# A state-space layer beside a dense Mish layer: the second block's first projection takes eight more tiles as seven products, its stages take turns, and its skip product goes to GpSimd

## The chip, the cores and the metric

The kernel runs on one core of a Trainium2 chip. The core has five engines that take their instructions in order, each from its own queue: TensorE (PE in the profile, with its weight loads as PEld), VectorE (DVE), ScalarE (ACT), GpSimd (POOL) and SyncE (SP), which only issues transfers (DMAs). They wait for each other through semaphores. The metric is the device time of one execution in microseconds (us). Before the change it is 592.89 us, the median of three runs (592.56 to 593.47).

## What is computed

The input x has 2048 rows of 1024 numbers (bf16). Each row is normalised to xn. Two layers are applied to xn and added to x:

```python
x = A_x
xn = _layernorm(x)
# A: a diagonal complex recurrence over the 2048 rows
Lam_bar = exp(exp(log_dt) * Lam)
Bu = xn @ B_bar.T                      # complex, 1024 states
h[t] = Lam_bar * h[t-1] + Bu[t]
A = 2 * real(h @ Cmat.T) + xn * Dskip  # xn * Dskip is the "skip product"
# B: a dense layer, 1024 -> 3584 -> 1024
g = xn @ w1 + b1
B = (g * tanh(softplus(g))) @ w2       # the activation is Mish
out = x + A + B
```

## The kernel before

The 2048 rows are taken in four blocks of 512, `blk` 0 to 3; the change is about `blk` 1, the second, which the code calls `FAST`. A block has these stages on TensorE: the *first projection* xn @ w1 (28 tiles of 128 columns, f = 0 to 27), the *input projection* xn @ B (eight groups j of 128 states, real and imaginary part), and the *second projection*, act @ w2, with the output product h @ C behind it in the same PSUM banks.

A plain tile of the first projection (`first_tile`, matmuls at L839) is eight matmuls of 128x512; ScalarE takes it out of PSUM with Mish (L847). A tile can also be taken as part of *seven products*: four tiles (a *quad*) by 1024 input rows by 512 block rows are cut in halves each way, and seven products of halves replace eight. Each of the seven, a *unit*, is eight matmuls of 128x256 (`w_product`, L984). Four of the seven need sums of weight quarters (`w_sums`, VectorE, L1134) and sums of xnT quarters (`sums_x`, VectorE, L1645, kept in `TT`). The scaled weights and the sums are written to DRAM (`wsd`) by DMAs from GpSimd's queue (`w_store`, L1113) and come back through the ring. After a unit its bank is copied or joined (`w_evacuate`: ScalarE L1004, VectorE L1007 and the joins L1021), and Mish follows later over four tiles at a time (`mish`, L862). The input projection is done the same way in pairs of groups, a, b, c and d, with the sums of B made on VectorE (`sums_B`, L1639, after `scale_B`, L1626) and held in SBUF; its products are at L914, its copies at L929, L931, L956 and L958, its joins at L939.

In `blk` 1 before: `TILES` are 20 plain tiles, and `OPEN` takes quads p and q (8 tiles, 14 units). `WHOLE` then does the input projection. These orders are written out by hand as strings, which `project_fast` reads one word at a time: a letter and a number.

- `a2`, `b1`, `c5`: product 2, 1, 5 of the input projection for pair a, b, c. Product 1 opens bank X, 2 opens Y and 5 opens Z; 6, 7 and 4 add to X, 3 adds to Z, and each of these must wait until what the bank held is copied or joined.
- `p1`, `q5`, `s2`, `w4`: the same for a quad of the first projection. `W_BANKS` names the three banks.
- `r0` to `r7`: `rotate_in(j)` on VectorE, three instructions (L877, L883, L885): a turn of 1.22 us and two of 0.42, each with two SBUF tensors.
- `k0`: one of the weight sums that are waiting in `steps`, with its store. `v5`: scale group 5's weights (ScalarE, L1119) and queue its sums. `n0`: load group 0's raw weights (GpSimd's queue, L1058). `P0`: one part of `sums_B(3)`. `g4`: one Mish pass. `l`: loads the next block's x (L390).
- `u4` to `u7`: the first rows of the second projection for one output bank (six matmuls, L1391).

The recurrence is done by `recur` on VectorE (two scans L1353 and a rotation per group). The skip product of `blk` 1 is `ln_skip` (VectorE, L590 and L592, eight instructions), called between the plain tiles by `side(f)`. The next block's row statistics are made by ScalarE (`next_stats`, L568 to L572), which writes into xn.

The *ring* has seven slots of 512 KB. Its loads are issued by SP in the fixed order of `items` (L440 for w1, w2 and C, L437 for pairs of units from `wsd`); each waits for its slot and, for units, for the stores of what it reads. `item_done` emits the next load each time an item is used up. All queues are emitted in the order in which the program calls the helpers, so what stands earlier in a queue holds up what stands behind it.

Of the kernel before, what the change touches and what calls it, by code (L numbers as in the profile page):

```python
# [5 lines left out]
ALU = mybir.AluOpType  # L6
# [3 lines left out]
P = 128  # L10
# [153 lines left out]
def build_kernel(nc, A_x, A_Lambda_re, A_Lambda_im, A_B_re, A_B_im, A_C_re, A_C_im,  # L164
# [18 lines left out]
    SPLIT = range(2, NB)  # L183
    GROUPS = ((0, 7), (7, NPL), (NPL, NPL + 8), (NPL + 8, NF), (12, 16), (16, 20))
# [17 lines left out]
    OPENS = [(REAL[QUADS.index(o[0])], int(o[1])) for o in OPEN.split() if o[0] in QUADS]  # L202
    O_ITEMS = [("w1", f // 2) for f in TILES[::2]] + [("ws", tuple(OPENS[i:i + 2])) for i in range(0, len(OPENS), 2)]

# [90 lines left out]
    srow = act[:, 24:26, :].rearrange("p f t -> p (f t)")  # L295
    srow0 = act[:, 26:28, :].rearrange("p f t -> p (f t)")
    base_st = nc.lookup_mloc(st).addr
# [288 lines left out]
    def ln_skip(blk, q):  # L586
# [241 lines left out]
    def item_done():  # L828
        n_item[0] += 1
        ring_load()  # L830

# [57 lines left out]

    def product(pr, n):  # L890

        X, Y, Z = (4 * ((pr + 1) % 2) + i for i in range(3))
        js = (2 * pr, 2 * pr + 1)
        lo, hi = slice(0, TH), slice(TH, TB)
        raw = {1: (0, 0, lo), 2: (0, NH, lo), 4: (1, NH, None), 3: (None, NH, hi)}
        bank = {1: X, 6: X, 7: X, 4: X, 2: Y, 5: Z, 3: Z}[n]
        opens = n in (1, 2, 5)
        for j in js:
            for k in range(NH):
                if n in (1, 2, 4):  # L900
                    w = BT[:, raw[n][0], j, raw[n][1] + k, :]
                    b_w = b_BT[j]
                elif n == 7:
                    w, b_w = BT16[:, 1, j, k, :], b_BT[j]
                else:
                    w, b_w = SS[:, j, {5: 0, 6: 1, 3: 2}[n], k, :], b_CT[j]
                if n in (1, 2, 3):
                    x, b_x = xnT[:, raw[n][1] + k, raw[n][2]], b_xnT
                else:
                    t = {5: 0, 6: 1, 7: 2, 4: 3}[n]  # L910
                    x, b_x = TT[:, t, k, :], [b_xn[t]]
# [52 lines left out]
    def w_product(blk, i, n):  # L964
        X, Y, Z = W_BANKS[i]
# [3 lines left out]
        s, half = n_item[0] % NRING, units.index((REAL[i], n))  # L969
        unit = ring[:, s, half * 1024:(half + 1) * 1024]  # L970
        if n not in (1, 2, 4):
            unit = unit.bitcast(f16)
        for j in range(2):
            for k in range(NH):
                if n in (1, 2, 3):
                    t0 = TH if n == 3 else 0
                    x, b_x = xnT[:, (0 if n == 1 else NH) + k, t0:t0 + TH], b_xnT
                else:
                    t = {5: 0, 6: 1, 7: 2, 4: 3}[n]
                    x, b_x = TT[:, t, k, :], [b_xn[t]]  # L980
                w = unit[:, k * 2 * P + j * P:k * 2 * P + (j + 1) * P]
# [8 lines left out]
    def w_evacuate(blk, i, n, keep):  # L990
        X, Y, Z = W_BANKS[i]
        at = REAL[i]
# [43 lines left out]
        if n == 4:  # L1036
            f0, dst, b_dst = w_out(blk, i, 1)
            whole(dst[:, :, 0:TH], b_dst, X, 1, AC if i in (0, 1, 3, 4) else VE)

# [4 lines left out]

    W_RAW = (("h", 0), ("h", 8), ("a", 0), ("h", 8), ("h", 0), ("h", 0), ("h", 8))

# [235 lines left out]
    def project_fast(blk, order, open_unit):  # L1282
        keep = {}
        for o in order.split():
# [9 lines left out]
            elif kind == "k":  # L1294
                if steps or later:
                    some(1)
            elif kind == "e":
                if later:
# [6 lines left out]
            elif kind == "P":  # L1305
                sums_B(3, (n,))
            elif kind == "S":
# [7 lines left out]
            elif kind == "n":  # L1315
                w_load(n)
            elif kind == "v":
                w_scale(n)
                w_sums(n, True)
            elif kind in QUADS:  # L1320
                w_product(blk, QUADS.index(kind), n)
                w_evacuate(blk, QUADS.index(kind), n, keep)
            else:
                product("abcd".index(kind), n)
                evacuate("abcd".index(kind), n, keep, kind in "ab")
        assert blk < NB - 1 or not (steps or later)
# [276 lines left out]
    def rows_fetch(h):  # L1603
        (AC if h else PO).dma(lambda e: e.dma_start(srow0[:, TB * h:TB * (h + 1)],
                                     scd[h].rearrange("p j -> (p j)").partition_broadcast(P)),
               DmaSem(nc, "d_srow%d" % h), reads=[b_scd[h]], writes=[b_actf[26 + h]])

    def rows_spread(h):
        vop(lambda e: e.tensor_copy(srow[:, TB * h:TB * (h + 1)].rearrange("p (j q) -> p j q", q=P),
                                    srow0[:, TB * h:TB * (h + 1)].rearrange("p (q j) -> p j q", q=P)),  # L1610
            reads=[b_actf[26 + h]], writes=[b_actf[24 + h]])

# [8 lines left out]
    def scale_B(pr, cis=(0, 1)):  # L1621
# [3 lines left out]
        for ci in cis:  # L1625
            vop(lambda e, ci=ci: e.tensor_tensor(  # L1626
                BT[:, ci, js, :, :], BT[:, ci, js, :, :], row.unsqueeze(2).to_broadcast([P, 2, NK, P]), op=ALU.mult),
                reads=b_B + [b_actf[24 + pr // 2]], writes=b_B)

# [11 lines left out]

    def sums_x(n, queue=PO):
        ll, lh, hl, hh = (xnT[:, a * NH:(a + 1) * NH, t * TH:(t + 1) * TH] for a in range(2) for t in range(2))
        a, b = ((lh, ll), (hh, TT[:, 0, :, :]), (hh, lh), (hl, TT[:, 1, :, :]))[n]
        queue.op(lambda e: e.tensor_tensor(TT[:, n, :, :], a, b, op=ALU.subtract),  # L1645
            reads=b_xnT + ([b_xn[0]] if n == 1 else [b_xn[1]] if n == 3 else []), writes=[b_xn[n]])

# [9 lines left out]
    for blk in range(NB):  # L1657

        def side(f):
            if blk:  # L1660
                if f < 3:
                    scale_B(0, (1,)) if f == 0 else None
                    rows_spread(1) if f == 1 else None
                    scale_B(f + 1)
                if f == 3:
                    w_sums(3)
                    w_scale(4)
                if f in (4, 5, 6, 7):
                    ln_skip(blk, f - 4)
                if f == 8:  # L1670
                    w_sums(4)
                if f == 10:
                    for n in range(4):
                        sums_x(n, VE)
                if f in (11, 12, 13):
                    sums_B(f - 11)
                if f == 15:
                    snaps_ready()
                if f == 19:
                    for q in range(NQ):  # L1680
                        load_x(PO, blk + 1, q, [b_actf[26]])
                    w_load(5)
                return
# [32 lines left out]
        elif blk:  # L1716
            project_fast(blk, OPEN + " " + WHOLE, open_unit)
        else:
            project_in()
# [81 lines left out]
        if near:  # L1801
            for q in range(NQ):
                ln_skip(blk + 1, q)
            for n in range(4):
                sums_x(n, VE)
        if 0 < blk < NB - 1:
# [4 lines left out]
        if blk == FAST - 1:  # L1811
# [50 lines left out]
```

## Time and profile before

| what | value |
|---|---|
| median of three runs | 592.89 us |
| the profiled execution's own time | 593.05 us |
| its span on the core | 591.8 us |
| TensorE busy | 588.3 us (99%) |
| VectorE busy | 494.7 us (84%) |
| ScalarE busy | 375.5 us (63%) |
| GpSimd busy | 158.0 us (27%) |

The stages around the change, in microseconds from the span's start, by TensorE's timeline:

| stage of `blk` 1 | from | to | VectorE busy | ScalarE busy |
|---|---|---|---|---|
| 20 plain tiles | 161 | 196 | 31.1 | 24.8 |
| quads p and q | 196 | 209 | 8.0 | 8.1 |
| input projection a to d | 209 | 236 | 19.8 | 16.8 |
| second projection | 236 | 281 | 44.1 | 28.8 |
| output product | 281 | 309 | 19.6 | 11.5 |

How to read it: a span is the time from the first to the last instruction of the profiled execution; the time of a run is a little longer. In the groups of instructions each row is a line of the kernel, an engine and a shape, with its count, its busy time and the mean of one in nanoseconds. In a timeline a row is the start, the length, the engine, the line, the operation, the tiles, the count, and the idle time before it. In the chain of work that ended last each piece is the start, the length and what ran.

### The profile page before, as it was taken

Reading aid. Unit: us, or ns where it says so; the run is one execution under the profiler, and the core shown is the slowest. Engines: PE = TensorE matmul, PEld = TensorE weight load, DVE = VectorE, ACT = ScalarE, POOL = GpSimd, SP = SyncE. Lnnn points to the kernel's source line nnn. Section 1 sums busy time; section 2 is a strip of 40 time slices with the busy share of each in tenths; the row PEclk is TensorE's granted clock in tenths of the full one; section 3 lists DMA queues with packets and bytes.
Section 4 is the critical chain, followed back from the end, with each engine's and each line's share of the span. In section 5 each row is a group of like instructions: output and inputs, shape, how many; then the busy total and the mean of one; then the engine's idle time right before and its main releaser. Section 6 shows DMA issues by size and latency. Waiting matters only on the chain.

```text
span 591.8 us, 9601 instructions
## 1 busy us (share of the span) xinstructions
PE 588.3 (99%) x3603; PEld 351.0 (59%) x3603; DVE 494.7 (84%) x732; ACT 375.5 (63%) x500; POOL 158.0 (27%) x225
## 2 busy tenths in 40 slices
PE   9999999999999999999999999999999999999998
PEld 8644444444444787444458888644446888854444
DVE  6998788999797758999947867998498669789996
ACT  4849994579494566953526577898351798892320
POOL 2899300223521334230112511144210123100000
DMA  9999999998868885799679959999998966989832
GB/s 242 315 235 262 219 177 247 309 383 254 237 204 312 282 306 180 266 298 233 218 258 393 410 178 292 352 332 276 276 293 277 396 236 231 329 326 320 287 125 72
DMA packets 116089, 160.32 MB, mean 271 GB/s; under 512 B 55850, under 2 KB 68906, under 8 KB 116042
## 3 DMA queue, kind: packets, MB, share of 16 engines
q1 hardware_dynamic: 96864, 102.85, 59.0%
q0 software_dynamic: 14112, 46.28, 23.0%
q10 hardware_dynamic: 5066, 10.57, 5.2%
q8 instruction: 29, 0.48, 0.3%
q14 instruction: 18, 0.15, 0.1%
HBM read 113.52 MB, written 34.08 MB: 249 GB/s over the span
## 4 chain that ended last, share of the span: by engine, by line
PE 98%; DMA 2%; SPq 0%; DVE 0%; issue 0%
PE ps L1391 43%; PE ps L984 15%; PE ps L914 12%; PE ps L839 12%; PE ps L1448 7%; PE ps L1337 5%; DMA ring<-wsd 2%; PE ps L656 1%; PE ps L665 1%; PE ps L618 1%; PE ps L496 0%; PE ps L1414 0%; PE ps L1422 0%; SPq L437 0%; PE ps L498 0%; PE ps L533 0%
## 5 line engine op out<-in xcount | busy, mean ns | idle before, releaser
L1391 PE MATMUL ps<-ring,act 128*128 128x512 bf16 x672 | 146.0, 379 | 0.0
L1391 PEld LDWEIGHTS ps<-ring,act 128*128 128x128 bf16 x672 | 65.8, 98 | 78.2
L1391 PE MATMUL ps<-ring,hT 128*128 128x512 bf16 x370 | 80.3, 379 | 0.0
L1004 ACT ACTIVATE snaps<-ps,par,cs 128x256 f32<-128x256 f32 x86 | 46.9, 562 | 46.0 <-PE ps L984 39.7
L839 PE MATMUL ps<-xnT,ring 128*128 128x512 bf16 x328 | 71.1, 379 | 0.0
L877 DVE TENSOR_TENSOR mt<-hT,tab 128x2048 bf16<-128x2048 bf16 (+1 forms) x56 | 68.4, 1222 | 1.4
L984 PE MATMUL ps<-TT,ring 128*128 128x256 f16 x512 | 63.6, 273 | 0.3 <-DMA ring<-wsd 0.3
L1391 PEld LDWEIGHTS ps<-ring,hT 128*128 128x128 bf16 x370 | 36.2, 98 | 43.7
L1161 POOL DMA_DIRECT2D w2d<-hb x42 | 29.9, 714 | 116.3 <-DVE hb L1189 70.5
L1353 DVE TENSOR_TENSOR_SCAN hT<-cs,qi,hT 128x512 bf16<-128x512 f32 x48 | 58.8, 1266 | 0.0
L839 PEld LDWEIGHTS ps<-xnT,ring 128*128 128x128 bf16 x328 | 32.1, 98 | 38.5
L984 PEld LDWEIGHTS ps<-TT,ring 128*128 128x128 f16 (+1 forms) x512 | 49.8, 98 | 7.1 <-DMA ring<-wsd 0.6
L1021 DVE SCALAR_TENSOR_TENSOR act<-ps,cs,snaps 128x512 bf16<-128x512 f32 x48 | 35.6, 748 | 21.0 <-PE ps L984 19.5
L984 PE MATMUL ps<-xnT,ring 128*128 128x256 bf16 x384 | 48.9, 273 | 0.0
L1113 POOL DMA_DIRECT2D wsd<-hb x42 | 22.8, 544 | 94.0 <-DVE hb L1134 58.3
L847 ACT ACTIVATE act<-ps,par 128x512 bf16<-128x512 f32 (+1 forms) x48 | 29.0, 665 | 19.4 <-PE ps L839 19.3
L984 PEld LDWEIGHTS ps<-xnT,ring 128*128 128x128 bf16 (+1 forms) x384 | 37.5, 98 | 5.2 <-issue 0.2
L1119 ACT ACTIVATE hb<-hb,cs 128x2048 bf16<-128x2048 bf16 x12 | 23.3, 1995 | 20.6 <-DVE cs L1108 15.9
L862 ACT ACTIVATE act<-act 128x4096 bf16<-128x4096 bf16 (+3 forms) x10 | 29.3, 2930 | 6.9 <-DVE act L1007 6.8
L939 DVE TENSOR_TENSOR hT<-ps,snaps 128x512 f16<-128x512 f32 x36 | 24.4, 688 | 10.5 <-ACT snaps L931 7.0
L1337 PE MATMUL ps<-xnT,BT 128*128 128x512 bf16 x128 | 27.8, 379 | 0.0
L1391 PE MATMUL ps<-CT,hT 128*128 128x512 bf16 x128 | 27.8, 379 | 0.0
(224 smaller groups left out, 979.2 us busy)
## 6 DMA issues: line engine op xcount, KB each, us to landing
ring<-in_B_w_dram SPq DMA_DIRECT2D x66, 512.0 KB, 5.7
ring<-wsd SPq DMA_DIRECT2D x112, 256.0 KB, 5.3
ring<-ctd SPq DMA_DIRECT2D x24, 512.0 KB, 4.8
ring<-w2d SPq DMA_DIRECT2D x24, 512.0 KB, 4.7
wsd<-hb POOLq DMA_DIRECT2D x42, 256.0 KB, 4.7
w2d<-hb POOLq DMA_DIRECT2D x42, 256.0 KB, 5.3
hb<-in_B_w_dram POOLq DMA_DIRECT2D x24, 256.0 KB, 5.5
ctd<-CT ACTq DMA_DIRECT2D x8, 512.0 KB, 6.4
```

The lines of the kernel that those rows point to most:

```text
L839: PE.mm(lambda e, k=k, w=w: e.matmul(ps[:, bank, :], lhsT=w, rhs=xnT[:, k, :], start=k == 0, stop=k == NK - 1), reads=[b_ring[s]] + b_xnT, ...
L862: aop(lambda e: e.activation(t, t, AF.Mish), reads=b, writes=b)
L877: vop(lambda e: e.tensor_tensor(mt[:], u.unsqueeze(1).to_broadcast([P, 2, 2, TB]), tab[:, :, j, :].unsqueeze(2).to_broadcast([P, 2, 2, TB] ...
L914: PE.mm(lambda e, w=w, x=x, o=o, begin=begin, end=end: e.matmul(ps[:, bank, o:o + TH], lhsT=w, rhs=x, start=opens and begin, stop=end, ski ...
L984: PE.mm(lambda e, w=w, x=x, o=o, begin=begin, end=end: e.matmul(ps[:, bank, o:o + TH], lhsT=w, rhs=x, start=opens and begin, stop=end, ski ...
L1004: aop(lambda e, o=o, p=p, j=j: e.activation(o, p, AF.Identity, scale=ig, bias=b1(f0 + j)), reads=[b_ps[b], b_par, b_ig], writes=b_dst)
L1021: vop(lambda e: e.scalar_tensor_tensor(out=dst, in0=bank(b), scalar=ig, in1=src, op0=ALU.mult, op1=ALU.add), reads=[b_ps[b], b_snap[k], b_ ...
L1161: PO.dma(lambda e: e.dma_start(w2d[at // 4][:, at % 4 * TB:(at % 4 + 2) * TB].rearrange("p (j t) -> p j t", j=2), t[:, :, d, :]), sem, rea ...
L1337: PE.mm(lambda e, j=j, ci=ci, k=k, bank=bank: e.matmul(ps[:, bank + ci, :], lhsT=BT[:, ci, j, k, :], rhs=xnT[:, k, :], start=k == 0, stop= ...
L1353: vop(lambda e, ci=ci, init=init: e.tensor_tensor_scan(out=hT[:, ci, j, :], data0=cj("r", j).to_broadcast([P, TB]), data1=hT[:, ci, j, :], ...
L1391: PE.mm(lambda e: e.matmul(ps[:, u, :], lhsT=lhsT, rhs=rhs, start=st_, stop=last, skip_group_check=blk == NB - 1), reads=reads, writes=[b_ ...
L1448: PE.mm(lambda e: e.matmul(ps[:, bank, :], lhsT=lhsT, rhs=rhs, start=st_, stop=end, skip_group_check=True), reads=[b_t, b_ring[s]], writes ...
```

## The change

Eight more tiles of `blk` 1 are taken as seven products: `TILES` keeps 12, and quads s and w (14 units, on groups 5 and 6) join p and q. `OPEN` is gone; the new `WHOLE` mixes the units of the input projection with those of the first projection, so that the input projection's pairs a and b come right after the 12 tiles. `F_BANKS` gives the quads of `blk` 1 banks of their own. The scaling of B, the weight sums of groups 3 and 4, the sums of x and half the sums of B are now called in one go after tile 0 (`side(0)`), the raw weights of groups 5 and 6 are loaded there, and group 5 is scaled after tile 7, into `act` 20 to 27. The tables are scaled four between the tiles and four between the units (`T4` to `T7`). The skip product of `blk` 1 becomes `skip_slow`: per quarter of the block two GpSimd instructions of 128x1024, `j0` after the units of a and b, and `j1` to `j3` among those of c and d. Because it needs xn for longer, the sums of x lie in `TT1`, on the x buffer of the block before, and the loads of the next block's x (`l0`) come behind w4, after which `TT1` is free. The ring emits a load of units only when its stores have been emitted (`ring_fill`). In `blk` 1 the copies of pairs a and b are made by ScalarE, not by VectorE.

```diff
-    TILES = [*range(12), *range(20, 28)]
-    WHOLE = ("v5 n6 a2 a1 b2 b1 a5 b5 a6 b6 a3 b3 a7 b7 c2 d2 a4 b4 k0 c5 c1 k0 d5 d1 k0 c6 c3 k0 d6 v6 d3 c7 d7 u7 r0 c4 u5 r1"
-             " d4 u6 r2 u4 n0 r3 r4 k0 k0 r5 k0 k0 n1 r6 r7")
-    OPEN = "p1 q1 p2 p5 P0 q5 q2 P1 p6 P2 q6 P3 p3 p7 q3 q7 p4 g4 q4 g5"
+    TILES = [*range(12)]
+    WHOLE = ("a2 a1 b2 b1 a5 b5 P4 P5 a6 b6 v6 P6 P7 a3 b3 P0 a7 b7 P1 j0 p1 q1 a4 b4 "
+             "k0 k0 p5 q5 k0 p2 q2 k0 p6 q6 P2 T4 p3 P3 q3 p7 q7 k0 c2 d2 p4 q4 T5 "
+             "k0 k0 k0 j1 c1 d1 r0 j2 c5 d5 T6 r1 c6 d6 T7 c3 d3 j3 c7 d7 r2 s1 s5 c4 d4 "
+             "r3 w1 w5 s2 w2 s6 w6 r4 s3 w3 s7 w7 u4 s4 w4 r5 u5 l0 u6 u7 n0 g4 g5 n1 r6 g6 g7 r7")
...
+    F_BANKS = ((3, 1, 2), (7, 5, 6), (7, 5, 6), (3, 1, 2))
...
+    TT1 = nc.alloc_sbuf_tensor_at("TT1", [P, 4, NH, TH], f16, offset=nc.lookup_mloc(xx).addr)
+
+    def diff(blk, n):
+        return (TT1[:, n, :, :], b_xx[0][n]) if blk == FAST else (TT[:, n, :, :], b_xn[n])
...
+    def skip_slow(blk, q):
+        xb, b_x = xx[:, blk % 2, q, :], b_xx[blk % 2][q]
+        pop(lambda e: e.tensor_tensor(xn[:, q, :], xn[:, q, :], dsk[:], op=ALU.mult),
+            reads=[b_xn[q], b_dsk], writes=[b_xn[q]])
+        pop(lambda e: e.tensor_tensor(xb, xb, xn[:, q, :], op=ALU.add), reads=[b_x, b_xn[q]], writes=[b_x])
...
+    def ring_fill():
+        while n_loaded[0] < min(n_item[0] + NRING, len(items)):
+            kind, g = items[n_loaded[0]]
+            if kind == "ws" and any(b_wsd[i][n - 1].writer is None for i, n in g):
+                return
+            ring_load()
...
-                evacuate("abcd".index(kind), n, keep, kind in "ab")
+                evacuate("abcd".index(kind), n, keep, kind in "ab" and blk != FAST)
...
         def side(f):
             if blk:
-                if f < 3:
-                    scale_B(0, (1,)) if f == 0 else None
-                    rows_spread(1) if f == 1 else None
-                    scale_B(f + 1)
-                if f == 3:
+                if f == 0:
+                    snaps_ready()
+                    scale_B(1, (1,))
                     w_sums(3)
-                    w_scale(4)
-                if f in (4, 5, 6, 7):
-                    ln_skip(blk, f - 4)
-                if f == 8:
+                    w_load(5)
+                    sums_B(0)
+                    for n in range(4):
+                        sums_x(blk, n)
+                    sums_B(1)
+                    w_load(6)
+                    rows_spread(1)
+                    scale_B(2)
                     w_sums(4)
-                if f == 10:
-                    for n in range(4):
-                        sums_x(n, VE)
-                if f in (11, 12, 13):
-                    sums_B(f - 11)
-                if f == 15:
-                    snaps_ready()
-                if f == 19:
-                    for q in range(NQ):
-                        load_x(PO, blk + 1, q, [b_actf[26]])
-                    w_load(5)
+                    scale_B(3)
+                if f in (1, 3, 4, 5):
+                    table_scale((1, 3, 4, 5).index(f))
+                if f == 7:
+                    w_scale(5)
+                    w_sums(5, True)
+                ring_fill()
                 return
...
-            scale_B(0, (0,))
+            scale_B(0)
+            scale_B(1, (0,))
             w_scale(3)
             rows_fetch(1)
-            for j in range(NJ):
-                table_scale(j)
+            w_scale(4)
```

More of the change, by code (lines that the diff above doesn't have):

```diff
@@ L183, in build_kernel @@
     SPLIT = range(2, NB)
-    GROUPS = ((0, 7), (7, NPL), (NPL, NPL + 8), (NPL + 8, NF), (12, 16), (16, 20))
-    TILES = [*range(12), *range(20, 28)]
-    WHOLE = ("v5 n6 a2 a1 b2 b1 a5 b5 a6 b6 a3 b3 a7 b7 c2 d2 a4 b4 k0 c5 c1 k0 d5 d1 k0 c6 c3 k0 d6 v6 d3 c7 d7 u7 r0 c4 u5 r1"
-             " d4 u6 r2 u4 n0 r3 r4 k0 k0 r5 k0 k0 n1 r6 r7")
-    OPEN = "p1 q1 p2 p5 P0 q5 q2 P1 p6 P2 q6 P3 p3 p7 q3 q7 p4 g4 q4 g5"
+    GROUPS = ((0, 7), (7, NPL), (NPL, NPL + 8), (NPL + 8, NF), (12, 16), (16, 20), (20, 24), (24, 28))
+    TILES = [*range(12)]
+    WHOLE = ("a2 a1 b2 b1 a5 b5 P4 P5 a6 b6 v6 P6 P7 a3 b3 P0 a7 b7 P1 j0 p1 q1 a4 b4 "
[3 rows of a table added]
     STEPS = ("p1 p5 p2 q1 q5 k0 k0 p6 q2 s1 k0 p7 s5 p3 k0 q6 s2 k0 p4 q7 k0 q3 k0 s6 q4 k0 m3 k0 g0 a2 a1 k0 s7 s3 k0 b2 b1 k0 s4 g1 m2 l0 a5 "
@@ L201, in build_kernel @@
     W_ITEMS = [("ws", tuple(UNITS[i:i + 2])) for i in range(0, len(UNITS), 2)]
-    OPENS = [(REAL[QUADS.index(o[0])], int(o[1])) for o in OPEN.split() if o[0] in QUADS]
+    OPENS = [(REAL[QUADS.index(o[0])], int(o[1])) for o in WHOLE.split() if o[0] in QUADS]
     O_ITEMS = [("w1", f // 2) for f in TILES[::2]] + [("ws", tuple(OPENS[i:i + 2])) for i in range(0, len(OPENS), 2)]
@@ L294, in build_kernel @@
     base_hb = nc.lookup_mloc(hb).addr
-    srow = act[:, 24:26, :].rearrange("p f t -> p (f t)")
-    srow0 = act[:, 26:28, :].rearrange("p f t -> p (f t)")
+    srow = act[:, 16:18, :].rearrange("p f t -> p (f t)")
+    srow0 = act[:, 18:20, :].rearrange("p f t -> p (f t)")
     base_st = nc.lookup_mloc(st).addr
@@ L888, in build_kernel, with product @@
     free_snaps = list(range(len(b_snap)))
-    def product(pr, n):
+    def product(blk, pr, n):
         X, Y, Z = (4 * ((pr + 1) % 2) + i for i in range(3))
@@ L910, in product @@
                     t = {5: 0, 6: 1, 7: 2, 4: 3}[n]
-                    x, b_x = TT[:, t, k, :], [b_xn[t]]
+                    x, b_x = diff(blk, t)
+                    x, b_x = x[:, k, :], [b_x]
                 o = (j - js[0]) * TH
@@ L964, in w_product @@
     def w_product(blk, i, n):
-        X, Y, Z = W_BANKS[i]
+        X, Y, Z = (F_BANKS if blk == FAST else W_BANKS)[i]
         bank = {1: X, 6: X, 7: X, 4: X, 2: Y, 5: Z, 3: Z}[n]
@@ L969, in w_product @@
         s, half = n_item[0] % NRING, units.index((REAL[i], n))
+        assert n_item[0] < n_loaded[0]
         unit = ring[:, s, half * 1024:(half + 1) * 1024]
@@ L979, in w_product @@
                     t = {5: 0, 6: 1, 7: 2, 4: 3}[n]
-                    x, b_x = TT[:, t, k, :], [b_xn[t]]
+                    x, b_x = diff(blk, t)
+                    x, b_x = x[:, k, :], [b_x]
                 w = unit[:, k * 2 * P + j * P:k * 2 * P + (j + 1) * P]
@@ L990, in w_evacuate @@
     def w_evacuate(blk, i, n, keep):
-        X, Y, Z = W_BANKS[i]
+        X, Y, Z = (F_BANKS if blk == FAST else W_BANKS)[i]
         at = REAL[i]
@@ L1037, in w_evacuate @@
             f0, dst, b_dst = w_out(blk, i, 1)
-            whole(dst[:, :, 0:TH], b_dst, X, 1, AC if i in (0, 1, 3, 4) else VE)
+            whole(dst[:, :, 0:TH], b_dst, X, 1, AC if blk == FAST or i in (0, 1, 3, 4) else VE)
     def w_unit(where):
@@ L1043, in w_unit @@
         return v[:, t:t + 2, :].rearrange("p f t -> p (f t)"), (b_hbf if kind == "h" else b_actf)[t:t + 2]
-    W_RAW = (("h", 0), ("h", 8), ("a", 0), ("h", 8), ("h", 0), ("h", 0), ("h", 8))
+    W_RAW = (("h", 0), ("h", 8), ("a", 0), ("h", 8), ("h", 0), ("a", 20), ("h", 8))
     def w_raw(i, ci, kh):
@@ L1296, in project_fast @@
                     some(1)
+                    ring_fill()
             elif kind == "e":
@@ L1305, in project_fast @@
             elif kind == "P":
-                sums_B(3, (n,))
+                sums_B(3 - n // 4, (n % 4,))
+            elif kind == "f":
+                scale_B(n)
+            elif kind == "T":
+                table_scale(n)
+            elif kind == "j":
+                skip_slow(blk, n)
             elif kind == "S":
@@ L1323, in project_fast @@
             else:
-                product("abcd".index(kind), n)
-                evacuate("abcd".index(kind), n, keep, kind in "ab")
+                product(blk, "abcd".index(kind), n)
+                evacuate("abcd".index(kind), n, keep, kind in "ab" and blk != FAST)
         assert blk < NB - 1 or not (steps or later)
@@ L1605, in rows_fetch @@
                                      scd[h].rearrange("p j -> (p j)").partition_broadcast(P)),
-               DmaSem(nc, "d_srow%d" % h), reads=[b_scd[h]], writes=[b_actf[26 + h]])
+               DmaSem(nc, "d_srow%d" % h), reads=[b_scd[h]], writes=[b_actf[18 + h]])
     def rows_spread(h):
@@ L1610, in rows_spread @@
                                     srow0[:, TB * h:TB * (h + 1)].rearrange("p (q j) -> p j q", q=P)),
-            reads=[b_actf[26 + h]], writes=[b_actf[24 + h]])
+            reads=[b_actf[18 + h]], writes=[b_actf[16 + h]])
     def keep_C(j):
@@ L1627, in scale_B @@
                 BT[:, ci, js, :, :], BT[:, ci, js, :, :], row.unsqueeze(2).to_broadcast([P, 2, NK, P]), op=ALU.mult),
-                reads=b_B + [b_actf[24 + pr // 2]], writes=b_B)
+                reads=b_B + [b_actf[16 + pr // 2]], writes=b_B)
     def sums_B(pr, parts=range(4)):
@@ L1640, in sums_B, with sums_x @@
                 reads=b_B + (b_C if n < 3 else []), writes=b_C if n < 3 else b_B)
-    def sums_x(n, queue=PO):
+    def sums_x(blk, n):
+        (o, b_o), (o0, b_0), (o1, b_1) = (diff(blk, i) for i in (n, 0, 1))
         ll, lh, hl, hh = (xnT[:, a * NH:(a + 1) * NH, t * TH:(t + 1) * TH] for a in range(2) for t in range(2))
-        a, b = ((lh, ll), (hh, TT[:, 0, :, :]), (hh, lh), (hl, TT[:, 1, :, :]))[n]
-        queue.op(lambda e: e.tensor_tensor(TT[:, n, :, :], a, b, op=ALU.subtract),
-            reads=b_xnT + ([b_xn[0]] if n == 1 else [b_xn[1]] if n == 3 else []), writes=[b_xn[n]])
+        a, b = ((lh, ll), (hh, o0), (hh, lh), (hl, o1))[n]
+        vop(lambda e: e.tensor_tensor(o, a, b, op=ALU.subtract),
+            reads=b_xnT + ([b_0] if n == 1 else [b_1] if n == 3 else []), writes=[b_o])
     def snaps_ready():
@@ L1660, in side @@
             if blk:
-                if f < 3:
-                    scale_B(0, (1,)) if f == 0 else None
-                    rows_spread(1) if f == 1 else None
-                    scale_B(f + 1)
-                if f == 3:
-                    w_sums(3)
-                    w_scale(4)
-                if f in (4, 5, 6, 7):
-                    ln_skip(blk, f - 4)
-                if f == 8:
-                    w_sums(4)
-                if f == 10:
-                    for n in range(4):
-                        sums_x(n, VE)
-                if f in (11, 12, 13):
-                    sums_B(f - 11)
-                if f == 15:
-                    snaps_ready()
-                if f == 19:
-                    for q in range(NQ):
-                        load_x(PO, blk + 1, q, [b_actf[26]])
-                    w_load(5)
+                if f == 0:
+                    snaps_ready()
+                    scale_B(1, (1,))
+                    w_sums(3)
+                    w_load(5)
[6 more added lines that the diff above has]
+                    scale_B(2)
+                    w_sums(4)
+                    scale_B(3)
[4 more added lines that the diff above has]
+                    w_sums(5, True)
+                ring_fill()
                 return
@@ L1716, in build_kernel @@
         elif blk:
-            project_fast(blk, OPEN + " " + WHOLE, open_unit)
+            project_fast(blk, WHOLE, open_unit)
         else:
@@ L1804, in build_kernel @@
             for n in range(4):
-                sums_x(n, VE)
+                sums_x(blk + 1, n)
         if 0 < blk < NB - 1:
```

1 line of the change is left out of this document (removed).

## The prediction

> **What bounds the kernel now.** I read the busy shares first, then the chain that ended last, then TensorE's timeline through the second block (blk 1 in the code), then VectorE's and GpSimd's timelines wherever both engines were at work.
>
> ```profile
> PE 588.3 (99%) x3603; PEld 351.0 (59%) x3603; DVE 494.7 (84%) x732; ACT 375.5 (63%) x500; POOL 158.0 (27%) x225
> ...
> PE 98%; DMA 2%; SPq 0%; DVE 0%; issue 0%
> ```
>
> TensorE (PE) has no idle time worth the name and carries 98% of the chain. So the time falls by the matmuls that are taken away, and rises by any wait of PE on another engine. The next lines are the second block in the chain in order of time (start, length, line, count).
>
> ```profile
> 161.25 34.55 PE ps L839 x160
> ...
> 197.19 9.50 DMA ring<-wsd
> 206.73 1.92 PE ps L984 x16
> ...
> 354.61 20.96 PE ps L984 x192
> ```
>
> 160 tile matmuls of 512 columns take 34.55 us: 0.2159 each, 1.727 a tile. 192 matmuls of 256 columns (24 units of eight, from blk 2) take 20.96: 0.8735 a unit. One unit's load came late; PE's timeline puts 0.32 us of idle time before 206.73, the only such gap in this block.
>
> The lines that decide the forecast are from the first block, where GpSimd (POOL) and VectorE (DVE) worked side by side.
>
> ```profile
> 23.96 1.26 POOL L740 TENSOR_TENSOR ph_h<-px,py 128x512 f32<-128x512 f32 x1
> 24.03 1.30 DVE L612 TENSOR_SCALAR cs<-cs 128x8 f32<-128x8 f32 x2
> ...
> 28.88 0.69 DVE L592 TENSOR_TENSOR xx<-xx,mt 128x1024 bf16<-128x1024 bf16 x1
> 29.11 1.58 POOL L740 TENSOR_TENSOR ph_h<-px,py 128x512 f32<-128x512 f32 x1
> 29.49 1.75 DVE L590 TENSOR_TENSOR mt<-xn,dsk 128x1024 bf16<-128x1024 bf16 x1
> ```
>
> L612 takes 0.17 us at its median and L590 0.68; while GpSimd ran an instruction with two SBUF tensors, both ended only after it (25.33 against 25.22, 31.24 against 30.69). In the second case GpSimd arrived at 29.11 while VectorE was in L592, lasted 0.32 longer than its usual 1.26, and still went ahead of VectorE's next instruction at 29.49. So the two engines take turns, one whole instruction each. GpSimd's instructions with one tensor do less: L592 at 27.27, inside a 2.04 us TENSOR_SCALAR of GpSimd, took 0.98 instead of 0.69.
>
> **The change part by part.** *Matmuls.* Eight tiles go: 64 x 0.2159 = 13.82 us. Fourteen units come: 14 x 0.8735 = 12.23. That is -1.59, all on the path. The 0.32 us wait goes too, as no unit is needed that early: -0.32.
>
> *Twelve tiles, then the input products.* PE starts a2 at 161.1 + 12 x 1.727 = 181.8. VectorE, free of block 0's output at 163.3, has in front of it five scalings of B (1.22 each), eight weight sums, eight sums of B and four of x (0.68 to 0.70), with a copy of 0.42 in all 20.4 us by its rows, to 183.7. The first join is wanted at 184.3 and a5, the first to need sums, runs at 185.3, with its sums written by 173: covered. ScalarE drops four of the eight table scalings before the tiles (1.08 each) and gains w_scale(4) there (3.9). It then needs the raw weights of group 5 by its tile 7. GpSimd issues them at 168 to 171; the loads of this kind took 6.4 us at the median and 8.8 at most, so they land at 176.5 to 179. Two scalings (3.9) and two tiles (1.3) later bank 1 is free, at 181.7 to 184.2; b2 wants it at 183.6. Cost 0 to 0.6; I take 0. The copies of a and b that move from VectorE to ScalarE (0.58 each, eight) lie in a stretch where it is half empty.
>
> *Loads.* SP issues 14 more units (256 KB) and four fewer w1 loads (512 KB). It stops at the store of q5, which VectorE makes at 179, until about 184; eleven issues of 0.42 and 4 us of landing later all seven p and q pairs are there by 193, p5 being wanted at 195.8. The second output projection's first rows (u4) need a 512 KB load whose slot is freed six units and four matmuls (6.1 us) earlier; blk 2 has the same distance before its u0 and PE's timeline has no gap there, though the median landing around it was 6.8. Cost 0 to 1.1; I take 0.
>
> *Later x loads.* They move behind w4 on GpSimd's queue, from 195 to 232 at the earliest; the group 0 and 1 weights queue behind them. The row statistics on ScalarE (10.2 us), which began at 236, then follow the four Mish passes (1.91 each). The square root was done at 253 and VectorE came for it at 259.6; now it is done at about 260, or later by as much as PE is. VectorE's 6.08 us of idle time before the block's output covers that: 0.
>
> *Skip product on GpSimd.* Eight instructions of 128x1024 with two SBUF tensors replace eight of VectorE (5.5 us with their overlaps, which covered nothing on the path). Their price from rows: GpSimd's TENSOR_TENSOR takes 0.198 us for 8 elements (L1374) and 1.268 for 512 (L740), so 2.12 ns an element and 2.36 us for 1024. The bounds are 1.27, if 16-bit elements go twice as fast, and twice L740, 2.54.
>
> Where they fall: j0 (two of them) goes in front of the stores of the k0 sums, at 194 to 199. VectorE has 8.4 us of work from 193.5 to p7's join, 201.9; two full turns make it 206.6, and p4 wants that join at 206.3. About 0.3. q7's join and the four w sums follow to 210.1. j1 to j3 (six) come behind the last of these sums' stores (0.55) and begin at 210.7. At that time VectorE is full: c1's and d1's joins (ScalarE's copies for them end at 211.8, behind p4, q4 and T5) end at 212.65, r0 and r1 take 2.05 each, and c3's join 0.69, to 217.45. PE wants c3's join for s5, which opens the same bank, at 161.1 + 20.73 + 41 x 0.8735 = 217.64. The slack is 0.2. Each rotation is three VectorE instructions with two SBUF tensors (1.22, 0.42, 0.42), so six in all before c3's join. Taking turns: j1's first product ends at 213.06 (0.4 after r0 wanted to start), and the five others go one after each of the next five VectorE instructions: 213.06 + 4.1 + 5 x 2.36 = 228.96, and the join ends at 229.66. **PE stands still for 12.0 us** (j0's 0.3 is inside it). c4 then waits for c7's join, two joins on: 0.4. What was queued behind all this on VectorE, r2 to r7 and the scans, is late by as much as PE is, and ScalarE and SP follow.
>
> *After the stop.* A PE that stood still may start slowly. The trace has one such start, its opening: 50 matmuls of 128 columns go at 0.107 to 0.117 us where later ones (L498) go at 0.056, 2.65 us lost. Ends 0 and 2.65; with no stop in this trace to choose by I take the middle, 1.3, less the 0.4 of c4 that it would hide: 0.9.
>
> The Trainium skill (TensorE: Matmul & The Clock Gate, What's actually happening) says that the array falls to half its clock after an idle window of about 3.4 us and needs another such window of work to come back. By it the start would cost some 1.7 us (an estimate from that page's window) and the sum would be 0.8 higher.
>
> Sum against the profiled execution's own 593.05 (span 591.8 and 1.25 around it): -1.59 - 0.32 + 12.0 + 0.4 + 0.9 = +11.4, so 604.4. The median of the three runs, 592.89, is 0.16 lower: **604.3**.
>
> **Rivals.** *Turns by rotation.* VectorE sends a rotation's three instructions through together and GpSimd gets in between rotations. For it: a rotation's third instruction is sent 0.08 us before the second ends. Against it: at 29.49 VectorE's next was sent 0.08 early as well and lost. Then r0 waits 0.4 and r1 2.36; c3's join ends at 220.2, a stop of 2.6, c4 0.4. Two of GpSimd's four remaining instructions fall beside joins, which read PSUM and one SBUF tensor; the others push r2 and r3, and s7's join, wanted by s4 at 232.4, ends at about 236.2: 3.8. -1.91 + 6.8 = +4.9: 597.8. GpSimd at 1.27 an instruction with full turns comes to the same: 5 x 1.27 less the slack, +4.3 to +5.
>
> *No turns to speak of (the other side).* If GpSimd's two-tensor instructions cost VectorE no more than its one-tensor ones did (about 0.3 each), or if GpSimd always waits, c3's join is late by at most 1.6 us. With nothing, c4's 0.3 is left: -1.91 + 0.3 = -1.6, 591.3, which is faster. It decides at 0.2 + 1.9 = 2.1 us of VectorE delay ahead of c3's join, less than one of GpSimd's six instructions; six at 0.3 give 1.8 and a time within 0.2% of before. For it: the one-tensor rows. Against it: both two-tensor rows.
>
> The Trainium skill (SBUF — State Buffer, SBUF: two separate sides) has it that the pair of ports is locked for a whole instruction by whichever engine starts first, and the other blocks fully. The two-tensor rows above agree (31.24 against 30.69); the one-tensor row does not (0.98, not 2.04). By that rule the time is 604.3, by the one-tensor row about 593.
>
> *More beside it.* The late load of group 5 (0.6), u4's load (1.1), the slow start (2.65) and GpSimd at 2.54 all at their upper ends: 608.5.
>
> **How the numbers follow.** Full turns at 2.1 to 2.54 us, 602 to 607: 0.48. Turns by rotation, or cheaper instructions, 594.2 to 602: 0.28. No turns: 0.19, of which 0.12 faster and 0.07 within 0.2% (1.2 us, about what a measurement of this kernel can tell from no change). Above 607: 0.05. So faster 0.12, same 0.07, slower 0.81. The range leaves out the no-turn cases and the far end: 594.0 to 608.0.
>
> **What would show it.** PE should have one long idle stretch after s1 (the 41st unit, about 218), ended by VectorE's join for c3 (L939 in the numbers of before), and the same in the chain. GpSimd should show eight TENSOR_TENSOR of 2.3 us or more, six from about 211, and VectorE's rotations there 2 us an instruction longer than 1.22 and 0.42. If those stay at 1.22 and 0.42 beside them, the forecast falls and 591.3 holds. If the stop lies elsewhere (b2 behind group 5's load, u4 behind its own), my covers were wrong. The matmul count should be 48 higher.

## The result and the profile after

The changed kernel takes 600.81 us, the median of four runs (600.59 to 601.42), beside 593.12 for the kernel before. The ratio is 1.0132 with a 95% interval of 1.0115 to 1.015: slower, by about 1.3%. The profiled execution took 601.42 us with a span of 600.2; before it was 593.05 and 591.8. The forecast was 604.3 with a range of 594 to 608.

The page of the changed kernel, busy shares and chain:

```profile
PE 588.9 (98%) x3651; PEld 356.5 (59%) x3651; DVE 500.1 (83%) x722; ACT 386.6 (64%) x518; POOL 179.3 (30%) x233
...
PE 95%; DVE 2%; DMA 1%; issue 1%; ACT 1%; SPq 1%; DVEq 0%
```

There are 48 more matmuls, as worked out, and the chain now runs over VectorE for 2% of the span. Who TensorE waited for behind the kernel's opening (line waited at, by whom, total us, times, longest):

```profile
PE ps L1007 <- DVE hT L960: 7.6, 1, 7.6
```

One wait, on one VectorE instruction (at the opening three more, of 0.2 to 1.0 us; the kernel before has the longest of them too): L960 is the input projection's join and L1007 is a unit of the first projection. TensorE's timeline shows the place (start, length, instruction, count, idle time before it):

```profile
216.92 1.04 PE L1007 MATMUL ps<-xnT,ring 128*128 128x256 bf16 x8
225.59 1.89 PE L1007 MATMUL ps<-TT,ring 128*128 128x256 f16 x8 [7.63 <-DVE hT L960]
227.27 3.62 PE L935 MATMUL ps<-TT,BT 128*128 128x256 f16 x16
230.68 1.15 PE L1007 MATMUL ps<-xnT,ring 128*128 128x256 bf16 x8
231.67 1.04 PE L1007 MATMUL ps<-TT,ring 128*128 128x256 f16 x8
```

The first row is s1, the second s5, then come c4 and d4, w1 and w5. s5 starts 7.63 us late. After the stop TensorE is slow: from s5's start to c4's are 1.68 us where a unit takes 0.8735, c4 and d4 together take 3.41, not 1.75, and w1 takes 0.99. That is 0.81 + 1.66 + 0.12 = 2.6 us more. The two stretches from s1 to w5 show it in the granted clock, which is 1.00 ahead of them and behind them (stretch, length, busy time of PE, PEld, DVE, ACT, POOL, then the clock):

```profile
216.90:225.60 8.70, 1.07 (x11) 0.72 (x10) 8.63 (x7) 0.00 (x0) 7.27 (x3) 0.72 0.29 110
225.60:231.70 6.10, 6.10 (x33) 4.46 (x34) 5.60 (x9) 3.43 (x6) 0.00 (x0) 0.57 0.29 86
```

This is the profiled execution, the slowest of the four. Its mean clock of 0.991 comes to some 10 us at half clock, and the 0.994 of the three others (600.59 to 600.90 us) to some 7, an estimate from the mean over the span. So 2.6 us is what the slow start cost in this execution, and the others, 0.5 to 0.8 us shorter, lost less.

What VectorE and GpSimd did meanwhile, first VectorE's timeline, then GpSimd's:

```profile
212.56 2.21 DVE L897 TENSOR_TENSOR mt<-hT,tab 128x2048 bf16<-128x2048 f16 x1
214.80 2.22 DVE L903 TENSOR_TENSOR hT<-mt 128x512 bf16<-128x512 bf16 x1
216.95 2.34 DVE L905 TENSOR_TENSOR hT<-mt 128x512 bf16<-128x512 bf16 x1
219.32 3.02 DVE L897 TENSOR_TENSOR mt<-hT,tab 128x2048 bf16<-128x2048 f16 x1
222.38 2.22 DVE L903 TENSOR_TENSOR hT<-mt 128x512 bf16<-128x512 bf16 x1
224.52 0.41 DVE L905 TENSOR_TENSOR hT<-mt 128x512 bf16<-128x512 bf16 x1
```

```profile
209.28 2.14 POOL L604 TENSOR_TENSOR xn<-xn,dsk 128x1024 bf16<-128x1024 bf16 x1
211.56 2.12 POOL L606 TENSOR_TENSOR xx<-xx,xn 128x1024 bf16<-128x1024 bf16 x1
213.64 3.11 POOL L604 TENSOR_TENSOR xn<-xn,dsk 128x1024 bf16<-128x1024 bf16 x1
216.89 2.12 POOL L606 TENSOR_TENSOR xx<-xx,xn 128x1024 bf16<-128x1024 bf16 x1
218.96 2.30 POOL L604 TENSOR_TENSOR xn<-xn,dsk 128x1024 bf16<-128x1024 bf16 x1
221.41 2.91 POOL L606 TENSOR_TENSOR xx<-xx,xn 128x1024 bf16<-128x1024 bf16 x1
```

These are r0 and r1, and j1 to j3. A rotation's instructions last 1.22, 0.42 and 0.42 us alone. Here the first lasts 1.00 longer, the next four 1.80, 1.92, 1.80 and 1.80 longer, and the last, which meets no GpSimd instruction, nothing: 8.32 us in all, for c3's join that stands behind them. GpSimd is held up as well: its third and its sixth last 3.11 and 2.91, not 2.12, because each waits for a turn of r0 or r1 (1.22) to end. Both lists read as one list of turns.

The sum closes: 8.32 less the slack of c3's join is the stop. The slack is 0.7 by what is left over, and 0.6 in the run without the skip product below, where that join ends at 217.32 and s5 starts at 217.90. In all -1.59 - 0.32 + 7.63 + 2.6 = +8.3, and the span grew by 8.4.

### The profile page after: what moved, and what is told of

It reads as the page before. It is cut to its first block, busy times and chain, and to the rows that moved or that the text cites. A ratio compares the mean times of both kernels' runs of the same rounds, so it can differ in the third digit from the quotient of the medians.

```text
span 600.2 us, 9754 instructions
## 1 busy us (share of the span) xinstructions
PE 588.9 (98%) x3651; PEld 356.5 (59%) x3651; DVE 500.1 (83%) x722; ACT 386.6 (64%) x518; POOL 179.3 (30%) x233
## 4 chain that ended last, share of the span: by engine, by line
PE 95%; DVE 2%; DMA 1%; issue 1%; ACT 1%; SPq 1%; DVEq 0%
PE ps L1421 42%; PE ps L1007 18%; PE ps L935 11%; PE ps L859 9%; PE ps L1478 7%; PE ps L1367 5%; DMA ring<-in_B_w_dram 1%; PE ps L678 1%; DVE mt L897 1%; PE ps L669 0%; DVE hT L905 0%; DVE hT L903 0%; DVE hT L960 0%; PE ps L1444 0%; ACT act L1027 0%
## 5 line engine op out<-in xcount | busy, mean ns | idle before, releaser
L1027 ACT ACTIVATE snaps<-ps,par,cs 128x256 f32<-128x256 f32 x98 | 53.6, 563 | 59.0 <-PE ps L1007 42.7
L1007 PE MATMUL ps<-TT,ring 128*128 128x256 f16 x576 | 72.1, 275 | 7.6 <-DVE hT L960 7.6
L1007 PEld LDWEIGHTS ps<-TT,ring 128*128 128x128 f16 (+1 forms) x576 | 56.5, 98 | 15.7 <-DVE hT L960 7.9
L1044 DVE SCALAR_TENSOR_TENSOR act<-ps,cs,snaps 128x512 bf16<-128x512 f32 x54 | 39.9, 748 | 21.2 <-PE ps L1007 19.4
L859 PE MATMUL ps<-xnT,ring 128*128 128x512 bf16 x264 | 57.3, 379 | 0.0
L1007 PE MATMUL ps<-xnT,ring 128*128 128x256 bf16 x432 | 54.6, 273 | 0.0
L1007 PEld LDWEIGHTS ps<-xnT,ring 128*128 128x128 bf16 (+1 forms) x432 | 42.4, 98 | 5.5
L859 PEld LDWEIGHTS ps<-xnT,ring 128*128 128x128 bf16 x264 | 25.8, 98 | 30.9
L882 ACT ACTIVATE act<-act 128x2048 bf16<-128x2048 bf16 (+3 forms) x12 | 32.8, 2756 | 6.8 <-DVE act L1030 6.8
L960 DVE TENSOR_TENSOR hT<-ps,snaps 128x512 f16<-128x512 f32 x36 | 23.9, 686 | 12.8 <-ACT snaps L952 10.4
L867 ACT ACTIVATE act<-ps,par 128x512 bf16<-128x512 f32 (+1 forms) x40 | 23.9, 655 | 10.6 <-PE ps L859 10.5
```

The source lines that it names most:

```text
L859: PE.mm(lambda e, k=k, w=w: e.matmul(ps[:, bank, :], lhsT=w, rhs=xnT[:, k, :], start=k == 0, stop=k == NK - 1), reads=[b_ring[s]] + b_xnT, ...
L882: aop(lambda e: e.activation(t, t, AF.Mish), reads=b, writes=b)
L1027: aop(lambda e, o=o, p=p, j=j: e.activation(o, p, AF.Identity, scale=ig, bias=b1(f0 + j)), reads=[b_ps[b], b_par, b_ig], writes=b_dst)
L1044: vop(lambda e: e.scalar_tensor_tensor(out=dst, in0=bank(b), scalar=ig, in1=src, op0=ALU.mult, op1=ALU.add), reads=[b_ps[b], b_snap[k], b_ ...
```

## The experiments

The theory: GpSimd's instructions with two SBUF tensors and VectorE's take turns, one whole instruction each, and that is the whole loss; TensorE's slow start is a consequence of standing still. The rivals: the new order alone overfills VectorE or ScalarE and the skip product only shares in it; any GpSimd work does it; it is a shared bandwidth and not turns; the slow matmuls have another reason.

**Without the skip product.**

```diff
             elif kind == "j":
-                skip_slow(blk, n)
+                pass
```

> The changed kernel with the second block's skip product left out altogether (x * Dskip is missing in that block's output); nothing else is different. Theory of turns (each two-tensor instruction of GpSimd holds up VectorE's two-tensor instruction for about 1.8 us, and that makes c3's join late): TensorE's stop before s5 is gone, the matmuls after it run at full pace, and what is left is the change of matmuls, -1.6, the wait of before that is gone, -0.3, and at most 0.3 before c4: 591.2 to 592.0 us. Rival, a full queue (the new order alone makes VectorE or ScalarE late and the skip product only shares the time): the stop before s5 stays at 5 us or more, 597 to 601 us.

591.04 us, ratio to before 0.9967 (0.9953 to 0.998). TensorE has no idle time between 180 and 245. The rotations are at 1.21 to 1.22, 0.43 and 0.42, and c3's join starts at 216.63 where it started at 224.85:

```profile
216.63 2.47 DVE L960 TENSOR_TENSOR hT<-ps,snaps 128x512 f16<-128x512 f32 x4
```

The time lies 0.2 us below the range expected. So the new order by itself costs nothing and brings what the count of matmuls says; the whole loss is the skip product's.

**The skip product on VectorE, at the same places.**

```diff
             elif kind == "j":
-                skip_slow(blk, n)
+                ln_skip(blk, n)
```

> The changed kernel with the skip product back on VectorE (two instructions of 0.69 us each quarter), called at the very same places, j0 to j3. Theory of turns: VectorE's rotations are back at 1.22 and 0.42 us; j0 and j1 fall into idle time of VectorE, j2 and j3 put 1.37 us each in front of c3's and c7's joins, where the slack is 0.2; TensorE stops for 1 to 2.5 us in all: 592.5 to 594.5 us, though VectorE has 5.5 us more to do than in the changed kernel. Rival, a full queue: more work on VectorE makes it worse than the changed kernel's 600.8 us.

593.69 us, ratio 1.0015 (0.9995 to 1.0036): as before the change, and 7 us better than with GpSimd, though VectorE has eight instructions more. TensorE's timeline:

```profile
184.06 1.91 PE L935 MATMUL ps<-xnT,BT 128*128 128x256 bf16 x16 [0.54 <-ACT act L867]
219.04 1.05 PE L1007 MATMUL ps<-TT,ring 128*128 128x256 f16 x8 [0.76 <-DVE hT L960]
221.56 1.92 PE L935 MATMUL ps<-TT,BT 128*128 128x256 f16 x16 [1.47 <-DVE hT L960]
```

The last two are s5 and c4, behind j2 and j3 on VectorE: 2.2 us, inside the 1 to 2.5 expected. After waits this short s5 takes 1.05 us to its end, as always. The first is b2, which waited for a tile that ScalarE took out late, since the raw weights of group 5 landed late there (ScalarE waited 3.28 us for them, 1.55 in the changed kernel) while TensorE came a little earlier (a2 at 181.61, 181.99 in the changed kernel). The forecast's 0 to 0.6 for that edit is real: it is on the edge.

**The skip product on VectorE, in its idle time.**

```diff
-             "k0 k0 p5 q5 k0 p2 q2 ...
+             "k0 k0 p5 q5 k0 j1 p2 q2 ...
-             "k0 k0 k0 j1 c1 d1 r0 j2 c5 d5 T6 r1 c6 d6 T7 c3 d3 j3 c7 d7 ...
+             "k0 k0 k0 j2 j3 c1 d1 r0 c5 d5 T6 r1 c6 d6 T7 c3 d3 c7 d7 ...
...
-                skip_slow(blk, n)
+                ln_skip(blk, n)
```

> As the one before, but j1 stands behind the third weight sum of group 5 (before p2) and j2 and j3 stand behind the last weight sum, before c1, where VectorE waited 2.9 us for ScalarE's copies in the changed kernel. Theory of turns: nothing is left that makes a join late but 0.3 before c4: 590.9 to 592.0 us, faster than both kernels. Rival, a full queue: 597 us or more.

591.43 us, ratio 0.9975 (0.9959 to 0.9991): faster than both kernels, by 0.25% beside the one before. VectorE's timeline in front of c1's join:

```profile
208.81 0.68 DVE L597 TENSOR_TENSOR mt<-xn,dsk 128x1024 bf16<-128x1024 bf16 x1
209.52 0.69 DVE L599 TENSOR_TENSOR xx<-xx,mt 128x1024 bf16<-128x1024 bf16 x1
...
211.81 1.29 DVE L960 TENSOR_TENSOR hT<-ps,snaps 128x512 f16<-128x512 f32 x2 [0.27 <-ACT snaps L952]
```

Half of the skip product, these two instructions and two more like them, fills the 2.92 us in which VectorE waited for ScalarE's copies in the changed kernel, and 0.27 of that wait is left. TensorE waits for nobody in this block.

**TensorE kept busy through the stop.**

```diff
-  ... c7 d7 r2 s1 s5 c4 d4 ...
+  ... c7 d7 r2 s1 f32 s5 c4 d4 ...
...
             elif kind == "f":
-                scale_B(n)
+                for i in range(n):
+                    PE.mm(lambda e: e.matmul(ps[:, 3, :], lhsT=xnT[:, 0, 0:P], rhs=xnT[:, 0, :], start=True, stop=True),
+                          reads=b_xnT, writes=[b_ps[3]], first=i == 0, last=i == n - 1)
```

> The changed kernel with 32 matmuls of 128x512 whose result nobody uses put in TensorE's queue behind s1 (6.9 us, bank 3), where it stood still for 7.6 us. Theory of a cold start (TensorE ran at half its clock after the stop because it had stood still; 2.6 us lost): a stop of about 0.7 us is left, s5, c4 and d4 take 0.87 us each, not 1.7, and the time falls by 2.2 to 2.6 us, to 598.2 to 598.7 us. Rival (the slow matmuls after the stop have another reason, or the filler makes c3's join later): 600.5 to 601.5 us.

The profiled executions differ by 2.4 us of span, 597.8 and 600.2, within the 2.2 to 2.6 expected. The medians differ by 1.8 only, 598.99 and 600.81, so the time misses the 598.2 to 598.7 expected by 0.3: the comparison of spans takes the changed kernel's slowest execution, the one that was at half clock longest. TensorE's timeline and the same stretches as above:

```profile
217.93 6.85 PE L1333 MATMUL ps<-xnT 128*128 128x512 bf16 x31
225.52 1.05 PE L1007 MATMUL ps<-TT,ring 128*128 128x256 f16 x8 [0.74 <-DVE hT L960]
226.72 1.92 PE L935 MATMUL ps<-TT,BT 128*128 128x256 f16 x16
```

```profile
216.90:225.60 8.70, 7.91 (x41) 3.84 (x41) 8.63 (x7) 0.02 (x1) 7.20 (x3) 1.00 0.32 120
225.60:231.70 6.10, 5.95 (x54) 5.10 (x55) 5.94 (x10) 5.38 (x10) 0.58 (x1) 1.00 0.28 93
```

s5 starts when it did, at 225.5, but c4 and d4 now end at full pace and the clock is 1.00. c4 starts 0.3 us later than s5's 0.87 us would have it, behind c7's join. So the slow matmuls are the price of having stood still, shown by taking the standing away and nothing else: 2.6 us in the profiled execution, less in the others.

**GpSimd's instructions with one tensor.**

```diff
-        pop(lambda e: e.tensor_tensor(xn[:, q, :], xn[:, q, :], dsk[:], op=ALU.mult), ...
-        pop(lambda e: e.tensor_tensor(xb, xb, xn[:, q, :], op=ALU.add), ...
+        pop(lambda e: e.tensor_scalar(xn[:, q, :], xn[:, q, :], 1.0, None, op0=ALU.mult), ...
+        pop(lambda e: e.tensor_scalar(xb, xb, 1.0, None, op0=ALU.mult), ...
```

> The changed kernel with GpSimd's eight two-tensor instructions replaced, one for one, by instructions with a single SBUF tensor of the same 128x1024 (xn times 1.0 and x times 1.0 in place; so the second block's skip product is left out). GpSimd has as much work at the same places, or more (about 3 us each by L736). Theory of turns, two tensors on both sides: VectorE's rotations go up by 0.3 us an instruction at most, as L592 did beside a one-tensor instruction; c3's join is late by 0 to 1.8 us and the time is 591 to 594 us. Rival (any instruction of GpSimd holds VectorE's two-tensor instruction to its end): six longer turns, a stop of 8 us or more, 600 to 607 us.

592.95 us, ratio 1.0016 (0.9989 to 1.0044), with the block's skip product left out. The profiled execution took 591.74, the least of ten; three of the ten took 596.9 to 597.3, two of them with a mean clock of 0.997, and what held these up no trace shows. GpSimd's instructions lasted 2.8 us each (one 3.4), longer than the two-tensor ones, and the stop before s5 was 0.60 us. VectorE's timeline for the same r0 and r1, and the GpSimd instruction that began before r0:

```profile
212.20 1.78 DVE L897 TENSOR_TENSOR mt<-hT,tab 128x2048 bf16<-128x2048 f16 x1
214.02 0.42 DVE L903 TENSOR_TENSOR hT<-mt 128x512 bf16<-128x512 bf16 x1
214.36 0.42 DVE L905 TENSOR_TENSOR hT<-mt 128x512 bf16<-128x512 bf16 x1
214.81 1.94 DVE L897 TENSOR_TENSOR mt<-hT,tab 128x2048 bf16<-128x2048 f16 x1
```

```profile
211.87 2.77 POOL L606 TENSOR_SCALAR xx<-xx 128x1024 bf16<-128x1024 bf16 x1 [0.15 <-POOL xn L604]
```

r0's L903 and L905 last 0.42 and start beside a GpSimd instruction that is still going (211.87 to 214.64). Where one of these instructions holds VectorE it does so once, by 0.56 and 0.72 here and by 0.72 and 0.87 at r2 and r3, not by its whole length. The rival's longer turns are not in this trace; the 0.3 expected was too low by half and more.

**Four turns in place of six.**

```diff
-             "k0 k0 k0 j1 c1 d1 r0 j2 ...
+             "k0 k0 k0 c1 d1 r0 j2 ...
```

> The changed kernel without j1 (one quarter of the second block has no skip product), so that four of GpSimd's instructions, not six, stand among the units of c and d. Theory of turns: 1.83 us less for each, so the stop before s5 goes from 7.6 to about 4.0 us, and the time to 596 to 597.5 us. Rival (one delay of a fixed size, whatever the number of instructions): the stop stays at 7 us or more.

597.04 us from two runs, with one quarter's skip product left out, ratio 1.0063 (1.0042 to 1.0085), with a stop of 4.04 us before s5: 7.63 less two instructions at 1.80. The rotations last 2.21, 2.23, 2.33, then 1.23, 0.42 and 0.42, so the loss ends with the fourth GpSimd instruction.

**Sixteen instructions of half the width.**

```diff
+        for h in range(2):
+            d = slice(h * 512, (h + 1) * 512)
             ... xn[:, q, d], dsk[:, d] ... xb[:, d] ...
```

> The changed kernel with each of GpSimd's eight instructions cut into two of half the width (128x512): sixteen instructions, the same work. Theory of turns (one whole instruction of GpSimd against one of VectorE): VectorE still has only six two-tensor instructions before c3's join, so at most six of GpSimd's go in between, and each now holds for 0.8 to 1.0 us: the stop before s5 falls to 4 to 5.5 us. Rival (GpSimd and VectorE share a bandwidth, so what counts is the amount of work): the stop stays at 7.5 us or grows with the overhead.

597.57 us from two runs (598.55, the profiled one, and 596.60), ratio 1.0072 (1.0048 to 1.0097), stop 4.01 us. VectorE's timeline for r0:

```profile
213.41 1.50 DVE L899 TENSOR_TENSOR mt<-hT,tab 128x2048 bf16<-128x2048 f16 x1
214.94 1.26 DVE L905 TENSOR_TENSOR hT<-mt 128x512 bf16<-128x512 bf16 x1
216.13 1.37 DVE L907 TENSOR_TENSOR hT<-mt 128x512 bf16<-128x512 bf16 x1
```

The same work in halves costs five of the six VectorE instructions of r0 and r1 about 0.9 each (1.26 - 0.42, 1.37 - 0.42; r1's are 2.06, 1.25 and 1.36), not 1.8, and the first one 0.3, and the stop falls with it. It is the length of one GpSimd instruction that counts, and how many of these meet a two-tensor instruction of VectorE in front of what TensorE wants. A shared bandwidth would have kept the stop.

## Why the prediction was right, point by point

- *The mechanism, its place and its sign: right.* One stop, before s5, ended by c3's join, because r0 and r1 took turns with j1 to j3. Runs without the skip product, with it on VectorE, with one-tensor instructions, with fewer and with shorter ones all move the stop as turns would. "Turns by rotation" fell: in the changed kernel GpSimd got in between the three instructions of a rotation. "No turns" fell as well. One of the two rows that it was read from is not quite what the prediction calls it: L612 has one tensor on VectorE's side. What the runs show is for two tensors on both sides.
- *-1.59 and -0.32: right.* The version with the skip product in VectorE's idle time has a span 1.6 us shorter than before, with 0.20 us of its own lost at the opening; the one without the skip product is 1.9 us shorter.
- *The stop of 12.0 us: 7.63.* Both of the term's factors were too large. The price of a turn was taken as GpSimd's full 2.36 us; such an instruction lasted 2.12 to 2.14 and held VectorE for 1.80 to 1.92. The number was five whole turns and 0.4 us of another; it was four and 1.0 us of another. GpSimd began j1 at 209.28, not 210.7, because j0 had made VectorE no later there: its three weight sums beside j0 took 5.74 us where they take 2.1, 3.6 more and not 4.7, and all of that fell into time in which VectorE waits for TensorE in the run without the skip product (the four weight sums ahead of j1 begin at 205.57, and at 205.66 there). So one instruction more of GpSimd passed beside ScalarE's copies and the joins of c1 and d1. The slack was 0.6 to 0.7, not 0.2.
- *c4's wait of 0.4 and p4's of 0.3: not there.* s5 ran slowly, and c7's join was ready when it ended; with the stop filled, c4 does wait 0.3. The prediction had said that a slow start would hide it.
- *The slow start of 0.9: 2.6.* The profiled execution shows the upper end that was named, the 2.65 us of the opening. The middle between the ends, 1.3, was too low for the other executions too, which lost some 1.8 to 2.1 if all that they are shorter by is the clock's (an estimate): the row of the one slow start in the trace was the better one. The Trainium skill (TensorE: Matmul & The Clock Gate, What's actually happening) has half the clock after an idle window of about 3.4 us, the full one after a busy window, and lets these windows run on without regard to when the kernel starts. The trace agrees that the clock is halved (units at 1.68 to 1.71 us) and that standing still does it, and the clock stays halved for a whole number of 3.41 us (see the last section). The 1.7 us worked out from one window was too little: TensorE worked at half clock from 225.59 to 230.90, 5.3 us.
- *The covers: right,* with one on the edge. Group 5's load let TensorE wait 0.54 us in one run and not in the others; u4's load and the later x loads cost nothing.

The two larger errors have opposite signs: 4.4 us too much for the stop, 1.7 too little for the slow start; with the 0.4 for c4 the forecast was 3.1 above +8.3. That it came so near is in part luck, since one error hid part of the other. Of the prediction's own cases, 600.81 lies in 594.2 to 602 (turns by rotation, or cheaper instructions, 0.28), not in 602 to 607 (full turns at 2.1 to 2.54 us, 0.48): the turns were full, but cheaper and one fewer.

The Trainium skill (SBUF — State Buffer, SBUF: two separate sides) locks the shared ports for a whole instruction when VectorE has two SBUF inputs and GpSimd's instruction reads SBUF. With two tensors on both sides the runs agree, at 1.80 to 1.92 us of a 2.12 to 2.14 us instruction; with one tensor on GpSimd's side they do not, at 0.56 to 0.87 us of 2.8.

## What to carry to other kernels

Work moved from a busy VectorE to an idle GpSimd is not off VectorE's path if both handle two SBUF tensors: look at what VectorE has queued beside it, count its two-tensor instructions ahead of the next thing that TensorE wants, and charge each with one GpSimd instruction, as long as GpSimd has one waiting. Here 5.5 us on VectorE, put into its own idle time, cost nothing, where the same work on GpSimd cost 8.3 us of VectorE's time in the wrong place. And a stop of TensorE can cost more than its length, since the matmuls after it start at half the clock: 2.6 us behind the stop of 7.63, and 1.7 and 2.5 us behind those of 4.04 (four turns) and 4.01 (half width).

## What was not expected of the hardware

- A two-tensor GpSimd instruction holds VectorE for less than it lasts: 1.80 to 1.92 us of 2.12 to 2.14 at 1024 elements, 0.83 to 0.95 of 1.15 at 512. The joins of c1 and d1, with one tensor in PSUM and one in SBUF, last 1.29 us for the two beside such an instruction, as without it.
- A one-tensor GpSimd instruction of 2.8 us holds VectorE's two-tensor instruction once, for 0.56 to 0.87 us; of r0 and r1 the instructions behind it keep their 0.42.
- After stops of 7.63, 4.04 and 4.01 us the next unit was slow (1.89, 1.83 and 1.89 us to its end); after stops of 0.6 to 0.8 us it was not (1.05), nor the two units after the stop of 1.47 us (1.92 together).
- The granted clock, read in stretches of 0.1 us, is 0.50 from 220.66 to 230.90 in the changed kernel, from 222.60 to 226.02 with four turns and from 221.15 to 227.98 with half width: 10.24, 3.41 and 6.83 us, three, one and two times 3.41. It fell 2.7, 4.1 and 2.3 us after the stop began. So two stops of nearly one length cost 1.7 and 2.5 us; the length alone does not tell the cost.
